# The last step of the inverse transform: three packed products of 128 rows in place of four of 96

## The chip, the core and the metric

The kernel runs on one core of one Trainium2 chip. The metric is the device time of one launch in microseconds. The kernel before takes 2950.87 us, the median of three runs (2947.91 to 2956.71).

## The reference

Two stages follow each other. The first filters a sequence of 3008 tokens of 256 channels in the frequency domain, for 8 batches; the second is a gated feed-forward layer over all 24064 tokens.

```python
X = np.fft.rfft(x, axis=1)                      # x: (8, 3008, 256)
y = np.fft.irfft(X * (filt_r + 1j * filt_i)[None], n=3008, axis=1).astype(np.float32)
t = y.reshape(8 * 3008, 256)
g = t @ w_gate                                  # (256, 1536)
v = t @ w_val                                   # (256, 1536)
out = (g / (1 + np.exp(-g)) * v) @ w_out        # (1536, 256)
```

All is in fp32 on the chip; the feed-forward weights come as float64 and are rounded to fp32 in the kernel.

## The kernel before

The transform of length 3008 = 47 x 64 is done in stages of small products: stage 1 over 47, stages 2a and 2b over 64 (with the filter between them), stage 3 over 47 back to tokens. Stages 1 and 2 of batch b+1, and stage 3 of the batch at hand, are laid as small pieces between the feed-forward products of batch b. All instructions of an engine stand in a fixed order.

A batch has four chunks of 752 tokens, each of two tiles of 376. A group is one chunk with one of three parts of the hidden width; so a batch has 4 x 3 = 12 groups. Stage 3 makes the tokens `y` of a chunk in four steps: two tiles `i`, each for two halves `cb` of the channels. Its input `t4` comes from DRAM, where stage 2b has put 48 rows (24 frequencies, real and imaginary) for each of 64 residues:

```python
N1, N2 = 47, 64
NS = 24
NR = 2 * N1          # 94 outputs of a pair of residues
NK = 4 * NS          # 96 rows of a pair: two blocks of 48
NH = 4               # pairs in a tile
TH = NH * NR         # 376
...
# the table of the last step, for a pair of residues h = 0, 1: block-diagonal, columns of the two mixed
wi = np.zeros((NS, 2, 2, N1, 2))
for h in range(2):
    wi[:, :, h, :, h] = v.transpose(2, 0, 1) / S
...
self.d2_rows = self.d2.rearrange("a (h n) c -> (a h) n c", h=2)    # d2: (48, 64, 256) in DRAM
...
def load(self, **kw):
    pin(nc.sync.dma_start(**kw))

def load_t4(self, k, i, part=None):
    if part is not None:
        ...                                     # first chunk of batch 0: into another buffer, in two parts
    else:
        t = t4pool.tile([NK, NH, C], FP32, name=f"t4_{self.b}_{k}_{i}", tag="t4")   # two buffers
        self.load(out=t, in_=self.d2_rows[:, ts(2 * k + i, NH), :])
    self.t4[k, i] = t

def stage3(self, k, step):
    if step == 0:
        self.y[k] = ypool.tile([128, 8, TQ], FP32, name=f"y_{self.b}_{k}", tag="y")
    i, cb = divmod(step, 2)
    ps = (self.bank if k == 0 else fbank)(f"pd_{self.b}_{k}_{step}")
    psv = ps.rearrange("p a b -> p (a b)")[:, 0:TH].rearrange("p (n r) -> p n r", n=NH)
    for n in range(NH):
        pin(nc.tensor.matmul(out=psv[:, n, :],
                             lhsT=self.t4[k, i][:, n, ts(cb, 128)],   # 96 x 128, stationary
                             rhs=wi_t, start=n == 0, stop=True,       # 96 x 94, moving
                             skip_group_check=True))
    yield
    ...                                         # ScalarE and VectorE copy and combine psv into y
```

Half of `wi_t` is zero: it takes both residues of a pair at once, and its columns come out in the order in which the tokens are wanted.

The loads of `t4` stand in SyncE's queue with everything else that it loads: the feed-forward weights of the next group (`wt_t`, four pieces a group, each rewritten when its last product is done), the input `x` of a later batch, filters and tables:

```python
chunk = {0: 1, 2: 2, 5: 3}.get(step)            # at the start of groups 0, 2 and 5 of a batch
if b and chunk:
    for i in range(2):
        cur.load_t4(chunk, i)
...
if nxt and (step, op) == (10, "A12" if b else "E23"):
    for i in range(2):
        nxt.load_t4(0, i)                       # the next batch's first chunk, in group 10
...
def reload_weights(g, piece):
    a, b = PIECES[piece]
    tc.keep_in_program_order(nc.sync.dma_start(out=wt_t[:, a:b], in_=w_dram[g, :, a:b]))
```

ScalarE starts the stores of stages 1 and 2b (`nc.scalar.dma_start`), between its copies.

The feed-forward products that surround these steps are of 188 and of 128 columns:

```python
for z in range(2):                              # lines 732 and 811 of the whole kernel
    pin(nc.tensor.matmul(out=ps[:, z], lhsT=self.wt[:, SLOT[p], z], rhs=rhs, ...))      # 128 x 188
...
pin(nc.tensor.matmul(out=self.tiles[at][:, t, :], lhsT=self.hs[i][:, HID[p], t0:t0 + 128],
                     rhs=wo_t[:, JB * q + i, WO[p], :], ...))                           # 128 x 128
```

Of the kernel before, what the change touches and what calls it, by code (L numbers as in the profile page):

```python
# [41 lines left out]
FP32 = mybir.dt.float32  # L42
# [6 lines left out]
B, S, C = 8, 3008, 256  # L49
# [4 lines left out]
N1, N2 = 47, 64  # L54
NS, NQ = 24, 64
NR = 2 * N1
NK = 4 * NS

NH = 4
# [50 lines left out]
PIECES = ((0, 7), (7, 14), (14, 20), (20, 26))  # L110


def dft_tables():
    n1, n2 = np.arange(N1), np.arange(N2)
    s, q = np.arange(NS), np.arange(NQ)
    ph = 2 * np.pi * (np.outer(n1, s) % N1) / N1
    w = np.stack([np.cos(ph), -np.sin(ph)], 1)
    wf = np.zeros((N1, 2, NS, 2, 2))
    wi = np.zeros((NS, 2, 2, N1, 2))

    v = np.stack([2 * np.cos(ph), -2 * np.sin(ph)], 0)
    v[0, :, 0], v[1, :, 0] = 1.0, 0.0
    for h in range(2):
        wf[:, h, :, :, h] = w.transpose(0, 2, 1)
        wi[:, :, h, :, h] = v.transpose(2, 0, 1) / S


    kap = np.where(q[:, None] < 32, s + N1 * q[:, None], s + N1 * (95 - q[:, None]))
    sg = np.where(q < 32, 1.0, -1.0)[:, None]
    th = 2 * np.pi * ((n2[:, None, None] * kap) % S) / S  # L130
    c, sn = np.cos(th), np.sin(th)
    d = np.zeros((2, N2, NS, 2, NQ))
    d[0, :, :, 0] = c.transpose(0, 2, 1)
    d[1, :, :, 0] = sn.transpose(0, 2, 1)
    d[0, :, :, 1] = (-sn * sg).transpose(0, 2, 1)
    d[1, :, :, 1] = (c * sg).transpose(0, 2, 1)
    d = d.reshape(128, NS, 128)
    de = np.stack([d, d.transpose(2, 1, 0)], 2)
    f32 = np.float32
    return (wf.reshape(NR, NK).astype(f32), wi.reshape(NK, NR).astype(f32),  # L140
            np.ascontiguousarray(de).astype(f32))


@with_exitstack
def kernel(
# [8 lines left out]
    out: bass.AP,  # L154
):
    nc = tc.nc
    wf_host, wi_host, de_host = dft_tables()
    wf_dram = nc.inline_tensor(wf_host, name="wf_tbl")
    wi_dram = nc.inline_tensor(wi_host, name="wi_tbl")
    de_dram = nc.inline_tensor(de_host, name="de_tbl").ap()  # L160
    unit_dram = nc.inline_tensor(np.eye(128, dtype=np.float32), name="unit_tbl")

    def pool(name, bufs, space=None):
        kw = {} if space is None else {"space": space}
        return ctx.enter_context(tc.tile_pool(name=name, bufs=bufs, **kw))

    cpool = pool("consts", 1)
    xpool = pool("xp", 2)
    t1pool = pool("t1", 2)
    t4pool = pool("t4", 2)  # L170
# [4 lines left out]

    wf_t = cpool.tile([NR, NK], FP32)
    wi_t = cpool.tile([NK, NR], FP32)

    wt_t = cpool.tile([128, NPR, 2, 128], FP32)
    y_t = cpool.tile([128, 3 * len(PAIRS), TQ], FP32)  # L180
# [25 lines left out]
    one = cpool.tile([128, 1], FP32)  # L206
# [15 lines left out]
    pin = tc.keep_in_program_order  # L222

    def add(eng, dst, a, b):
        return eng.tensor_tensor(out=dst, in0=a, in1=b, op=ALU.add)  # L225
# [50 lines left out]
    def load_weights(i):  # L276
        if i in raws or i >= len(weights):
            return
        if i < N_EARLY:
            raws[i] = early_raw(i)  # L280
        elif spot_of(i) is not None:
            raws[i] = bits(4 * 7 * 128 + 512 * spot_of(i))
        else:
            raws[i] = rpool.tile([128, 2, 128, 2], U32, name=f"raw_{i}", tag="raw", bufs=2)
        pin(nc.sync.dma_start(out=raws[i], in_=weights[i][0]))
# [169 lines left out]
    def bank(name):  # L455
        return wps.tile([128, 512], FP32, name=f"w{name}", tag="w")
# [4 lines left out]
    def idle(t, banks, n):  # L461

        for ps in banks:
            pin(nc.tensor.matmul(out=ps[:, 0:n], lhsT=t[:, 0:128], rhs=t[:, 0:n],
                                 start=True, stop=True))

    class Spectral:
# [59 lines left out]
        def load_t4(self, k, i, part=None):  # L527
            if part is not None:

                t = f0[0:NK, ts(i, NH), :]  # L530
                r = (slice(0, 64), slice(64, NK))[part]
                self.load(out=t[r], in_=self.d2_rows[r, ts(i, NH), :])
            else:
                t = t4pool.tile([NK, NH, C], FP32, name=f"t4_{self.b}_{k}_{i}", tag="t4")
                self.load(out=t, in_=self.d2_rows[:, ts(2 * k + i, NH), :])
            self.t4[k, i] = t

        def bank(self, name):
# [93 lines left out]
# [4 lines that stand above are left out]
            i, cb = divmod(step, 2)  # L636
            ps = (self.bank if k == 0 else fbank)(f"pd_{self.b}_{k}_{step}")
            psv = ps.rearrange("p a b -> p (a b)")[:, 0:TH].rearrange("p (n r) -> p n r", n=NH)
            for n in range(NH):
                pin(nc.tensor.matmul(out=psv[:, n, :],  # L640
                                             lhsT=self.t4[k, i][:, n, ts(cb, 128)],
                                             rhs=wi_t, start=n == 0, stop=True,
                                             skip_group_check=True))
            yield

            y = self.y[k]

            def tokens(part, parts):
                return y[:, part:part + parts].rearrange("p t (r n) -> p n (t r)", n=NH)

            if cb == 0:
                pin(nc.scalar.copy(out=tokens(2 * i, 2), in_=psv))
                return
            for t in range(2):
                a, c = 2 * i + t, psv[:, :, ts(t, N1)]
                b, v, k = tokens(a, 1), tokens(4 + a, 1), KS[a]
                if k == 0:
                    pin(nc.scalar.copy(out=v, in_=c))
                elif k == -1:
                    pin(add(nc.vector, v, c, b))  # L660
                else:
                    pin(nc.vector.scalar_tensor_tensor(
                        out=v, in0=b, scalar=-float(k), in1=c, op0=ALU.mult, op1=ALU.add))
# [172 lines left out]
    def run(piece):  # L836
        for _ in piece:
            pass

    with tc.tile_pool(name="start", bufs=1) as spool0:  # L840
# [12 lines left out]
        n = 0  # L853
# [34 lines left out]
        for u in range(N_TWO + lag):  # L888
            if u < N_TWO:
                spec.turn(u + 2)  # L890
                step = spec.stage2a(u)
                next(step)
                next(step)
                preparation.tick(0, 2 * (u < N_TWO - 2), hold=True)
                run(step)
                preparation.release()
                spec.real_part(u + 1)
            if u >= lag:
                if u == N_TWO:
                    idle(zero, [bank("idle")], 512)  # L900
                elif u > N_TWO:
                    preparation.tick(0)
                run(spec.stage2b(u - lag))
            if u == 6:
                pin(nc.sync.dma_start(out=wi_t, in_=wi_dram.ap()))
                for i in range(8, N_EARLY):
                    load_weights(i)
            if u == N_TWO - 1:
                for i in range(2):
                    spec.load_t4(0, i, 0)  # L910
# [7 lines left out]
        for p in ("A13", "A01"):  # L918
            at = SLOT[p]
# [32 lines left out]
    def order_of(b):  # L952

        steps = [divmod(step, NG) for step in range(NCHUNK * NG)]
        if b == 0:
            steps[:NT * NG] = [(k, g) for g in range(NG) for k in range(NT)]
        return steps
# [44 lines left out]
    for b in range(B):  # L1002
# [8 lines left out]
        one = [nxt.stage1(u) for u in range(N_ONE)] if nxt else []  # L1011
# [24 lines left out]
        for step in range(NCHUNK * NG + (b == B - 1)):  # L1036
            ghost = step == NCHUNK * NG
            k, g = order_of(b)[min(step, NCHUNK * NG - 1)]
# [15 lines left out]
            for place, token in enumerate(SCHEDULE):  # L1054
# [5 lines left out]
                if op[0] == "t":  # L1060
                    n = int(op[1])
                    ps = pieces_before if old else pieces
# [59 lines left out]
```

## Time and profile before

| what | before |
|---|---|
| span of the profiled run | 2946.9 us |
| TensorE busy, records | 2911.7 us, 20264 |
| weight loads | 2816.1 us |
| VectorE, ScalarE, GpSimd busy | 1929.3, 1609.9, 1579.8 us |
| mean granted TensorE clock | 0.998 |
| records of stage 3's products (`pd`, line 640) | 992, of 128.3 us busy |
| loads of `t4` through SyncE | 62, of 384 KB each |
| all DMA packets, bytes | 217452, 558.57 MB |

In the profile PE is TensorE's products, PEld its weight loads, DVE VectorE, ACT ScalarE, POOL GpSimd and SPq the queue in which SyncE starts its DMAs. Every fp32 product leaves two records of each kind. Names of tiles stand without buffer numbers: `t` is `t4`, `d` the DRAM tensors between the stages, `pd` the result of stage 3, `pa`, `pb` and `pc` those of stages 1, 2a and 2b, `wk`, `wa`, `we` those of the hidden products and `wA`, `wF`, `wG` those of the output products. Busy times of overlapping records add up to more than the time that they take, so the distance between two starts on the timeline says more than a length.

### The profile page before, as it was taken

How to read it: one execution, taken by the hardware profiler on the slowest of the kernel's cores; microseconds unless marked ns; L12 is line 12 of the kernel's file. 1: busy time of each engine (PE TensorE's matmuls, PEld its weight loads, DVE VectorE, ACT ScalarE, POOL GpSimd, SP SyncE). 2: the span in 40 equal slices, each digit the busy share in tenths (PEclk: the TensorE clock that was granted, in tenths of full speed). 3: DMA queues.
4: the chain of work that ended last, by engine and by line, in shares of the span. 5: the costliest groups of instructions: out<-in, count | busy, mean ns of one | idle time of the engine just before them, and what ended most of it. 6: DMA issues, size and time to landing. Idle time of an engine off the chain costs nothing.

```text
span 2946.9 us, 57623 instructions
## 1 busy us (share of the span) xinstructions
PE 2911.7 (99%) x20264; PEld 2816.1 (96%) x20264; DVE 1929.3 (65%) x4384; ACT 1609.9 (55%) x4208; POOL 1579.8 (54%) x1759
## 2 busy tenths in 40 slices
PE   7999999999999999999999999999999999999999
PEld 5889999999999999999999999999999999999999
DVE  6888765576655676557765667656666566766666
ACT  6775455545555555555455554555555555555554
POOL 3876655556444655455554456454564545555453
PEclk9999999999999999999999999999999999999999
DMA  8677855575555655556646566556665565644442
GB/s 232 212 255 245 299 188 184 174 229 180 178 179 185 222 186 171 182 188 200 213 152 194 188 195 212 162 176 203 194 199 171 177 211 190 201 138 152 148 129 88
DMA packets 217452, 558.57 MB, mean 190 GB/s; under 512 B 29962, under 2 KB 107642, under 8 KB 217166
## 3 DMA queue, kind: packets, MB, share of 16 engines
q1 hardware_dynamic: 171326, 485.59, 51.5%
q10 hardware_dynamic: 36912, 45.43, 4.6%
q0 software_dynamic: 8928, 23.89, 2.3%
q8 instruction: 162, 2.65, 0.4%
q14 instruction: 124, 1.02, 0.1%
HBM read 459.73 MB, written 95.05 MB: 188 GB/s over the span
## 4 chain that ended last, share of the span: by engine, by line
PE 94%; DVE 1%; POOL 1%; DMA 1%; issue 0%; ACT 0%; SPq 0%; DVEq 0%; POOLq 0%
PE wa L732 24%; PE wA L811 17%; PE wk L732 16%; PE we L732 12%; PE wG L811 9%; PE wF L811 4%; PE pd L640 4%; PE pa L548 3%; PE pc L620 2%; PE pb L588 2%; DMA y_t<-yt 0%; POOL y_t L225 0%; DVE h L779 0%; POOL wt_t L225 0%; POOL wt_t L228 0%
## 5 line engine op out<-in xcount | busy, mean ns | idle before, releaser
L732 PE MATMUL wa<-y_t,wt_t 128*128 128x188 f32 x4464 | 880.2, 323 | 5.2 <-issue 1.4
L732 PEld LDWEIGHTS wa<-y_t,wt_t 128*128 128x128 f32 x4464 | 730.0, 190 | 30.1 <-issue 17.3
L225 POOL TENSOR_TENSOR h<-h 128x376 f32<-128x376 f32 x190 | 183.1, 985 | 787.1 <-DVE h L779 777.5
L811 PE MATMUL wA<-wo_t,h 128*128 128x128 f32 x4608 | 577.7, 275 | 2.5 <-DVE o L225 2.0
L811 PEld LDWEIGHTS wA<-wo_t,h 128*128 128x128 f32 x4608 | 562.9, 192 | 16.2 <-issue 10.4
L732 PE MATMUL wk<-y,wt_t 128*128 128x188 f32 x2976 | 567.9, 324 | 0.0
L228 POOL TENSOR_TENSOR h<-h 128x376 f32<-128x376 f32 x570 | 553.5, 993 | 0.5
L732 PEld LDWEIGHTS wk<-y,wt_t 128*128 128x128 f32 x2976 | 479.2, 191 | 25.9 <-issue 19.8
L228 DVE TENSOR_TENSOR we<-we,m 128x376 f32<-128x376 f32 x576 | 318.6, 556 | 196.9 <-PE we L732 138.4
L732 PE MATMUL we<-y_t,wt_t 128*128 128x188 f32 x2232 | 431.5, 323 | 1.4 <-ACT we L763 1.4
L732 PEld LDWEIGHTS we<-y_t,wt_t 128*128 128x128 f32 x2232 | 369.4, 190 | 1.8 <-ACT we L763 1.7
L228 POOL TENSOR_TENSOR D<-f,f 128x376 f32<-128x376 f32 x288 | 281.0, 989 | 104.6 <-ACT f L747 103.9
L232 DVE SCALAR_TENSOR_TENSOR y<-wk,c 128x376 f32<-128x376 f32 x480 | 245.1, 543 | 133.8 <-ACT we L763 83.2
L767 ACT COPY m<-wa 128x376 f32<-128x376 f32 x576 | 272.0, 472 | 88.2 <-PE wa L732 87.0
L774 ACT ACTIVATE g<-wa 128x188 f32<-128x188 f32 x576 | 188.1, 327 | 190.6 <-PE wa L732 182.6
L811 PE MATMUL wG<-wo_t,h 128*128 128x128 f32 x2304 | 288.3, 275 | 0.6 <-DVE o L225 0.6
L811 PEld LDWEIGHTS wG<-wo_t,h 128*128 128x128 f32 x2304 | 281.4, 192 | 0.8 <-DVE o L225 0.8
L774 ACT ACTIVATE u<-we 128x188 f32<-128x188 f32 x576 | 189.0, 328 | 168.8 <-DVE we L228 149.9
L747 ACT ACTIVATE f<-wk 128x376 f32<-128x376 f32 x288 | 139.3, 484 | 235.4 <-PE wk L732 214.3
L751 ACT COPY c<-wk 128x376 f32<-128x376 f32 x288 | 136.0, 472 | 226.0 <-PE wk L732 226.0
L754 DVE SCALAR_TENSOR_TENSOR x<-wk,f 128x376 f32<-128x376 f32 x192 | 104.6, 545 | 235.8 <-PE wk L732 230.0
L763 ACT COPY we<-y 128x376 f32<-128x376 f32 x480 | 224.1, 487 | 33.7 <-DVE h L779 14.7
(142 smaller groups left out, 3915.9 us busy)
## 6 DMA issues: line engine op xcount, KB each, us to landing
wt_t<-w_all SPq DMA_DIRECT2D x174, 896.0 KB
wt_t<-w_all SPq DMA_DIRECT2D x174, 768.0 KB
t<-d SPq DMA_DIRECT2D x62, 384.0 KB
d<-t ACTq DMA_DIRECT2D x112, 192.0 KB
lent<-de_tbl SPq DMA_DIRECT2D x84, 256.0 KB
lent<-in_filt_r_dram SPq DMA_DIRECT2D x336, 64.0 KB
lent<-d SPq DMA_DIRECT2D x84, 256.0 KB
d<-lent ACTq DMA_DIRECT2D x84, 256.0 KB
```

What stands on the lines that cost most here:

```text
L225: return eng.tensor_tensor(out=dst, in0=a, in1=b, op=ALU.add)
L228: return eng.tensor_tensor(out=dst, in0=a, in1=b, op=ALU.subtract)
L232: return nc.vector.scalar_tensor_tensor(out=dst, in0=a, scalar=-1.0, in1=b, op0=ALU.mult, op1=ALU.subtract)
L640: pin(nc.tensor.matmul(out=psv[:, n, :], lhsT=self.t4[k, i][:, n, ts(cb, 128)], rhs=wi_t, start=n == 0, stop=True, skip_group_check=True))
L732: pin(nc.tensor.matmul(out=ps[:, z], lhsT=self.wt[:, SLOT[p], z], rhs=rhs, start=start and z == 0, stop=True, skip_group_check=True))
L747: pin(act.mul(self.small(f"f{i}", f"f{i}", 1), t[f"k{i}"], -1.0))
L751: pin(act.copy(out=self.small(f"c{i}", f"c{i}", 1), in_=t[f"k{i}"]))
L754: pin(v.scalar_tensor_tensor(out=dst, in0=t[f"k{j}"], scalar=-1.0, in1=t[f"f{i}" if j == 3 else f"D{at}"], op0=ALU.mult, op1=ALU.add))
L763: pin(act.copy(out=self.bank(f"e{at}"), in_=t[f"y{at}"]))
L767: pin(act.copy(out=self.small(f"m{at}", "m", 4), in_=t[f"a{at}"]))
L774: pin(act.activation(out=self.small(op, "g", 3, 1)[:, 0], in_=ps[:, 1], func=AF.Silu))
L811: pin(nc.tensor.matmul(out=self.tiles[at][:, t, :], lhsT=self.hs[i][:, HID[p], t0:t0 + 128], rhs=wo_t[:, JB * q + i, WO[p], :], start=star ...
```

## The change

A tile of four pairs has eight blocks of 48 rows, 384 rows in all, and that is three times 128. The change packs them: three tiles of 128 rows, where two blocks are cut in two parts (32 and 16 rows) that lie in neighbouring tiles, and whose partial results TensorE adds up in PSUM. So three products with all 128 rows take the place of four with 96, and the zeros of the table go. A new table `back_t` holds, for each of the three tiles, the block-diagonal coefficients: 3, 4 and 3 blocks of 47 columns. The order of the tokens in PSUM is the same as before, so a product now writes every second element. The load of a tile, one DMA before, is seven: for each packed tile one with two whole blocks, and one for each part.

The first chunk of batch 0 keeps the old way (`back = self.b or k`). The table is loaded once, at the start.

```diff
+BACK = (((0, 0, 0, 48), (1, 48, 0, 48), (2, 96, 0, 32)),
+        ((4, 64, 0, 48), (5, 112, 0, 16), (2, 0, 32, 16), (3, 16, 0, 48)),
+        ((5, 0, 16, 32), (6, 32, 0, 48), (7, 80, 0, 48)))
+BACK_AT = (0, 3 * N1, 7 * N1)
...
+    one = wi[:, :, 0, :, 0].reshape(2 * NS, N1)
+    back = np.zeros((128, 10 * N1))
+    for tile_, first in zip(BACK, BACK_AT):
+        for i, (_, row, a, rows) in enumerate(tile_):
+            back[row:row + rows, first + N1 * i:first + N1 * (i + 1)] = one[a:a + rows]
...
+    back_t = cpool.tile([128, 10 * N1], FP32)
...
-                t = t4pool.tile([NK, NH, C], FP32, name=f"t4_{self.b}_{k}_{i}", tag="t4")
-                self.load(out=t, in_=self.d2_rows[:, ts(2 * k + i, NH), :])
+                t = t4pool.tile([128, len(BACK), C], FP32, name=f"t4_{self.b}_{k}_{i}", tag="t4")
+                n = (2 * k + i) * NH
+                for j, tile_ in enumerate(BACK):
+                    whole = [(blk, row) for blk, row, _, rows in tile_ if rows == 2 * NS]
+                    for blk, row, a, rows in tile_:
+                        if rows < 2 * NS:
+                            at = blk // NH * 32 + n + blk % NH
+                            self.load(out=t[row:row + rows, j], in_=self.d2[a:a + rows, at])
+                    (blk, row), (blk2, row2) = sorted(whole, key=lambda w: w[1])
+                    at, at2 = [z // NH * 32 + n + z % NH for z in (blk, blk2)]
+                    both = self.d2[:, at:at2 + 1:at2 - at]
+                    self.load(out=t[row:row + 4 * NS, j], in_=both.rearrange("a n c -> n a c"))
...
-            for n in range(NH):
+            flat = ps.rearrange("p a b -> p (a b)")
+            back = self.b or k
+            for j in range(len(BACK) if back else 0):
+                first = BACK_AT[j]
+                cols = back_t[:, first:first + N1 * len(BACK[j])]
+
+                if j == 1:
+                    rows = flat[:, 1:2 * 187 + 1].rearrange("p (z y) -> p z y", z=2)[:, :, ::2]
+                else:
+                    at = j // 2 * (2 * N1 + 1)
+                    rows = flat[:, at:at + 6 * N1 - 1:2]
+                pin(nc.tensor.matmul(out=rows, lhsT=self.t4[k, i][:, j, ts(cb, 128)], rhs=cols,
+                                     start=j == 0, stop=True, skip_group_check=True))
+            for n in range(0 if back else NH):
                 pin(nc.tensor.matmul(out=psv[:, n, :],
...
+                pin(nc.sync.dma_start(out=back_t, in_=back_dram.ap()))
```

## The prediction

> **What bounds the kernel now.** I read the page's totals first, then its chain that ended last:
>
> ```profile
> PE 2911.7 (99%) x20264; PEld 2816.1 (96%) x20264; DVE 1929.3 (65%) x4384; ACT 1609.9 (55%) x4208; POOL 1579.8 (54%) x1759
> PE wa L732 24%; PE wA L811 17%; PE wk L732 16%; PE we L732 12%; PE wG L811 9%; PE wF L811 4%; PE pd L640 4%; PE pa L548 3%; PE pc L620 2%; PE pb L588 2%; DMA y_t<-yt 0%; POOL y_t L225 0%; DVE h L779 0%; POOL wt_t L225 0%; POOL wt_t L228 0%
> ```
>
> TensorE is the chain; the product that the change touches (pd, line 640) holds 4% of it. Next the table of busy time by stretch, for the start and one whole batch (columns: stretch, length, then busy time and count of TensorE, its weight loads, VectorE, ScalarE and GpSimd, then clock, DMA share, GB/s):
>
> ```profile
> 0.00:100.00 100.00, 81.15 (x448) 64.05 (x449) 71.78 (x144) 66.29 (x144) 46.44 (x66) 0.98 0.81 222
> 820.00:1180.00 360.00, 360.00 (x2513) 349.38 (x2513) 229.22 (x525) 193.21 (x505) 188.81 (x204) 1.00 0.59 189
> ```
>
> Of a batch's 360 us TensorE is busy for 360.00, so in batches 1 to 7 every ns taken from TensorE's stream should come off the span, unless something new makes it wait. Only the start has idle time.
>
> A record's busy time is no measure here, as records overlap: I take the distance between starts. TensorE's timeline around one changed product (start, length, operation, records):
>
> ```profile
> 1019.63 1.50 PE L811 MATMUL wF<-wo_t,h 128*128 128x128 f32 x12
> 1020.96 1.03 PE L620 MATMUL pc<-lent 128*128 128x256 f32 x4
> ...
> 1026.35 0.80 PE L732 MATMUL wk<-y,wt_t 128*128 128x188 f32 x4
> 1026.99 1.03 PE L640 MATMUL pd<-wi_t,t 96*128 96x94 f32 x8
> 1027.85 1.53 PE L811 MATMUL wA<-wo_t,h 128*128 128x128 f32 x12
> 1029.22 0.80 PE L732 MATMUL wk<-y,wt_t 128*128 128x188 f32 x4
> ```
>
> Each product leaves two records. Width 128: 1.33 us for 12, so 111 ns a record. Width 188: 0.64 for 4, so 160 ns. Width 256: the 4 pc records take 0.87, some 216 ns. That is a straight line of about 0.81 ns per column and record. At 94 columns it would give 84 ns, but pd's 8 records take 0.86 us, and the 12 records after them 1.37 instead of 1.33: 0.89 to 0.90 us for 8, again 111 ns. So pd pays for 128 columns of weights whatever it streams: it stands on a floor.
>
> **What the Trainium skill says.** "TensorE: Matmul & The Clock Gate", section "LDWEIGHTS (loading the stationary operand)": a load's time goes with the columns of the stationary operand, not its rows. The trace agrees: the 96-row load of pd takes 193 ns, the 128-row load of wA 192. Its section "Back-to-back issue gap" says the spacing is set by both load and matmul; the floor above shows it. "PSUM — Partial Sum Buffer", section "Specifications (TRN2)", says of 8-byte cachelines: "any non-contiguous AP slows matmuls significantly". The new products write every second fp32 element; no product of the kernel before does so, so no trace here shows its size. "DMA: Bandwidth & Descriptors", section "Anatomy of one DMA — SWDGE (gpsimd) path", puts a fixed cost of about 2.0 us on a DMA; the output stores on GpSimd's queue land 2.3 to 2.5 us after issue, which agrees.
>
> **The change part by part.**
>
> *Products.* The four-block path stays for the first chunk of batch 0; the other 31 chunks of 4 steps, 124 steps, change. Each lost 4 products of 96 rows by 94 columns, half of them against zeros, and gets three of 128 rows with 141, 188 and 141 columns. Before: 8 records at 111 ns, 889 ns. After: 141 columns are 111 + 13 x 0.81 = 122 ns, above the floor; so 4 x 122 + 2 x 160 = 808 ns. More columns (470 for 376), but fewer loads: 81 ns less. 124 x 81 = **10.0 us** less on TensorE, 248 of 20264 records fewer. Nearly all of it lies in full batches (16 steps, 1.3 us of 360 each).
>
> *Loads of t4.* One load of 384 KB becomes seven, with runs of 1 KB for 4 KB. SyncE's queue, around the load of a batch's first chunk:
>
> ```profile
> 1118.06 0.32 SPq L376 DMA_DIRECT2D wt_t<-w_all  x1
> 1127.83 0.80 SPq L479 DMA_DIRECT2D t<-d  x2
> 1128.73 8.83 SPq L376 DMA_DIRECT2D wt_t<-w_all  x3
> ```
>
> An issue costs about 0.40 to 0.45 us. A chunk's two loads become 14, some 6.3 us for 0.9; 31 x 12 = 372 more issues are about 160 us of SyncE over the span. Does it delay TensorE? The tile of the load at 1127.83 is first used at 1140.36, 12.5 us later; the one at 807.10 at 821.96; those at 867.74 and 958.60 over 60 us later. The first half (7 issues, 3.2 us, plus 2.5 to land) is there after 5.7 us, the second after 8.9, and its use is 12 us behind the first's. The weight reloads behind them (line 376) start 5.4 us later; a piece is rewritten once its last product is done and first read some 22 us later by the order of the schedule, and 896 KB at 190 GB/s take 4.7 us, so some 12 us are left. All hidden.
>
> *ScalarE.* In the built program a DMA of SyncE or ScalarE takes one of eight semaphores in turn and waits for the DMA eight before it. With 14 loads in a row, the next one or two of ScalarE's stores wait for a small load that now goes out late. Load at 1167.12, ScalarE's next store at 1171.55: the load eight before is about the eighth or ninth of 14, out at 1167.1 + 8 x 0.45 = 1170.7, landed near 1173, so ScalarE stands still for about 1.5 us. It is busy 54% of the batch. I estimate up to 0.3 us on TensorE, perhaps 10 times in all: 2.5 us.
>
> *The start.* Chunk 1's loads go out at 70.99, first use 78.49; seven issues and landing end at 76.7, just in time, while the raw weight load behind (71.98) comes 5.4 us later and a second set at 94.02 does the same. TensorE waits here already. I take 1.5 us, and nothing for the new 240 KB table.
>
> Sum: -10.0 + 2.5 + 1.5 = -6.0 us: 2944.9.
>
> **The rivals.** (1) *The strided output slows the product.* If it doubled the record, a step would take 1616 ns for 889: +0.73 x 124 = +90 us, 3041. For it: the skill's sentence, and that the kernel before kept outputs contiguous at the price of zeros. Against: fp32 streams a column in 0.81 ns, about two clocks of 2.4 GHz (the rate in the skill's "Back-to-back issue gap"), so there may be time to write each element by itself; that is a guess. I give it one chance in six, and a smaller slowdown one in ten. (2) *The loads become the wait*: ScalarE's stop reaches TensorE in full, 1.5 us x 31 = 46 us, 2997. For it: SyncE's queue is in order and shared with weight reloads. Against: the slack above, and ScalarE's 46% idle time. (3) *The gain is hidden anyway*, as another engine is the bound: 2951. Against: 360.00 of 360. (4) *Narrow records cost less than I think*: if pd really costs only the 0.86 us seen, the saving is 52 ns x 124 = 6.4 us, and the result 2948.
>
> **Range and chances.** The most that can be won is 10 us, 0.3%, so faster by 2% is all but out. Low end: all 10 us and a little of the start, 2938. High end: a mild form of (1) or (2), 30 to 40 us. A loss over 2% (59 us) needs rival 1 nearly whole.
>
> **What would show it.** Right: pd's records 6 a step, at 4 x 122 + 2 x 160 ns between starts, a batch some 1.3 us shorter than before, TensorE still at 360 of 360. The strided write would show as pd records over 200 ns apart; the loads as TensorE waits after ScalarE, on t (pd waiting for a DMA) or on wt_t. A longer start alone would show in the first 150 us. I would be wrong if the spacing of pd isn't what the line through wider products gives.

## The result, and the profile after

The changed kernel takes 3054.65 us (median; 3052.44 to 3059.9) against 2951.31: a ratio of 1.0351, 95% interval 1.033 to 1.0372. It is slower by 103 us, far above the range that I gave.

The page of the changed kernel, its totals and its chain (the lines that answer to those of before):

```profile
PE 2933.3 (96%) x20016; PEld 2825.5 (93%) x20016; DVE 1931.9 (63%) x4384; ACT 1610.1 (53%) x4208; POOL 1579.5 (52%) x1759
PE wa L771 22%; PE wA L850 15%; PE wk L771 15%; PE we L771 11%; PE wG L850 8%; PE wF L850 4%; DMA t<-d 3%; PE pd L676 3%; PE pa L574 3%; PE pb L614 2%; DMA lent<-de_tbl 2%; PE pc L646 2%; DMA x<-in_x_dram 2%; DMA lent<-d 1%; SPq L495 1%; DMA d<-lent 1%
```

TensorE has 248 records fewer, as foreseen, and yet is busy for longer, and at 96% no longer all of the time. DMA holds 11% of the chain, where it held 1%: transfers of `t`, of `lent` (the tables and inputs of stage 2) and of `x` (the input of stage 1) stand in it now.

The products themselves did what they should. TensorE's timeline around one of them (start, length, operation, records):

```profile
1065.67 0.80 PE L771 MATMUL wk<-y,wt_t 128*128 128x188 f32 x4
1066.31 0.96 PE L676 MATMUL pd<-back_t,t 128*128 128x141 f32 x6
1067.11 1.50 PE L850 MATMUL wA<-wo_t,h 128*128 128x128 f32 x12
1068.45 0.80 PE L771 MATMUL wk<-y,wt_t 128*128 128x188 f32 x4
```

Six records take 0.80 us, where the four products took 0.86, and the twelve that follow take 1.34 in place of 1.37. That is the 808 ns of the prediction, so the strided output adds nothing to it that can be seen.

The time went into waits of TensorE. Its three largest, and its wait for `t` itself, in the view of who waited for whom (total us, times, longest):

```profile
PE pb L614 <- DMA lent<-d: 38.0, 8, 9.2
PE pa L574 <- DMA x<-in_x_dram: 24.1, 6, 4.1
PE wa L771 <- ACT m L806: 16.8, 14, 1.9
PE pd L676 <- DMA t<-d: 4.3, 3, 1.8
```

In the kernel before, no wait of TensorE comes to 5 us in all. One of the waits for `lent`, on the timeline with what follows it (in brackets the idle time before, and what ended it):

```profile
1010.03 0.80 PE L771 MATMUL we<-y_t,wt_t 128*128 128x188 f32 x4
1016.02 2.04 PE L614 MATMUL pb<-lent 128*128 128x256 f32 x4 [5.19 <-DMA lent<-d]
1017.86 1.46 PE L771 MATMUL wa<-y_t,wt_t 128*128 128x188 f32 x4
1019.11 1.11 PE L771 MATMUL we<-y_t,wt_t 128*128 128x188 f32 x4
1020.06 0.80 PE L771 MATMUL wa<-y_t,wt_t 128*128 128x188 f32 x4
```

The wait costs more than itself. After it the four pb records take 1.84 us to the next start in place of 0.87, the next four 1.25 and then 0.95 in place of 0.64: some 1.9 us more, until the pace is back. The table by stretch (columns as in the prediction) has the granted clock, third from the end, at about half in that time and back at full from 1020 on:

```profile
1016.00:1018.00 2.00, 1.98 (x5) 1.64 (x6) 0.00 (x0) 0.00 (x0) 0.00 (x0) 0.50 0.97 399
1018.00:1020.00 2.00, 2.00 (x9) 2.00 (x8) 1.74 (x3) 0.00 (x0) 0.00 (x0) 0.57 1.01 308
1020.00:1022.00 2.00, 2.00 (x18) 2.00 (x17) 1.16 (x3) 1.74 (x5) 1.08 (x2) 1.00 0.47 110
```

Over the whole span the mean granted clock falls from 0.998 to 0.985.

Why was the transfer late? SyncE's queue of the changed kernel ahead of that wait (start, length of the issue with its waits, transfer, number):

```profile
990.27 0.34 SPq L392 DMA_DIRECT2D wt_t<-w_all  x1
990.67 10.68 SPq L495 DMA_DIRECT2D t<-d  x14
1001.91 1.26 SPq L392 DMA_DIRECT2D wt_t<-w_all  x1
1003.22 2.03 SPq L495 DMA_DIRECT2D lent<-de_tbl  x1
1005.35 2.35 SPq L495 DMA_DIRECT2D lent<-in_filt_r_dram  x4
1009.85 2.55 SPq L495 DMA_DIRECT2D lent<-in_filt_i_dram  x2
1013.08 0.39 SPq L495 DMA_DIRECT2D lent<-d  x1
```

The 14 loads take 10.68 us, not 6.3, and the loads behind them go on slowly too. The last line is the transfer that TensorE waits for. SyncE's queue itself stands still for earlier loads of `t` (a DMA waits for the one eight before it), which it never does in the kernel before:

```profile
SPq L495 <- DMA t<-d: 66.8, 84, 2.1
```

So the place of the loss is plain; its cause may be the number of issues (theory A), the short runs of 1 KB (theory B), or the products and their order in time (theory C).

### The profile page after: what moved, and what is told of

The parts are those of the page before. It is cut to its first block, busy times and chain, and to the rows that moved or that the text cites. A ratio compares the mean times of both kernels' runs of the same rounds, so it can differ in the third digit from the quotient of the medians.

```text
span 3052.3 us, 57570 instructions
## 1 busy us (share of the span) xinstructions
PE 2933.3 (96%) x20016; PEld 2825.5 (93%) x20016; DVE 1931.9 (63%) x4384; ACT 1610.1 (53%) x4208; POOL 1579.5 (52%) x1759
## 2 busy tenths in 40 slices
DMA packets 238803, 558.84 MB, mean 183 GB/s; under 512 B 33326, under 2 KB 134942, under 8 KB 238514
## 4 chain that ended last, share of the span: by engine, by line
PE 85%; DMA 11%; DVE 1%; SPq 1%; POOL 1%; ACT 1%; issue 1%; ACTq 0%; DVEq 0%; POOLq 0%
PE wa L771 22%; PE wA L850 15%; PE wk L771 15%; PE we L771 11%; PE wG L850 8%; PE wF L850 4%; DMA t<-d 3%; PE pd L676 3%; PE pa L574 3%; PE pb L614 2%; DMA lent<-de_tbl 2%; PE pc L646 2%; DMA x<-in_x_dram 2%; DMA lent<-d 1%; SPq L495 1%; DMA d<-lent 1%
## 5 line engine op out<-in xcount | busy, mean ns | idle before, releaser
L771 PE MATMUL wa<-y_t,wt_t 128*128 128x188 f32 x4464 | 887.6, 325 | 19.2 <-ACT m L806 16.8
```

## The experiments

**One load a tile.** If the eight blocks of a tile lie one after another in DRAM, their 384 rows are just what the three packed tiles want, and one DMA brings them, in runs of 1 KB as in the changed kernel. Stage 2b then writes its rows in another order (the columns of its table are swapped to suit), which also makes its stores runs of 2 KB.

```diff
-    ...                                    # the seven loads
+    rows = self.d2.rearrange("(t m) a c -> t (m a) c", t=8)[2 * k + i]     # 384 successive rows
+    self.load(out=t, in_=rows.rearrange("(j p) c -> p j c", p=128))
```

> The packed products stay, but stage 2b's rows lie in DRAM so that a packed tile is 384 successive rows, and one DMA of 1 KB runs loads it. Theory A (the 14 issues of a chunk in SyncE's in-order queue hold up the loads of x and of stage 2 behind them): TensorE's waits of some 12 us a batch go, the saving of 0.06 to 0.09 us a step stays, some 8 to 11 us under the kernel before: 2940 to 2944. Theory B (the 1 KB runs in place of 4 KB make the transfers slow, whatever their number): about as slow as the changed kernel, 3040 to 3055. Theory C (the strided products are at fault, and the waits only follow): also above 3040.

Measured: 2940.68 us, ratio to the kernel before 0.9972 (0.9963 to 0.9982). The products keep their gain, and runs of 1 KB are not at fault: theories B and C fall. By theory A the next run had to be slow.

**The same rows, seven loads.** Only the number of DMAs differs from the run before.

```diff
-    self.load(out=t, in_=rows.rearrange("(j p) c -> p j c", p=128))
+    for j, cuts in enumerate(((0, 32, 128), (0, 16, 32, 128), (0, 32, 128))):
+        for a, z in zip(cuts, cuts[1:]):
+            self.load(out=t[a:z, j], in_=rows[128 * j + a:128 * j + z])
```

> The same order of rows in DRAM as in the run with one load, but the tile is loaded by seven DMAs of the sizes that the changed kernel has. Theory A: as slow as the changed kernel, 3040 to 3060, the number of DMAs being the only difference to the run with one load. Theory B: the same as the run with one load, whatever that is.

Measured: 2939.6 us, ratio 0.9969 (0.9956 to 0.9983). So seven DMAs of the same sizes cost nothing, and theory A falls as well. The queue of this run shows what differs:

```profile
955.85 7.22 SPq L496 DMA_DIRECT2D t<-d  x14
963.94 0.34 SPq L394 DMA_DIRECT2D wt_t<-w_all  x1
964.32 0.43 SPq L496 DMA_DIRECT2D lent<-de_tbl  x1
964.85 1.87 SPq L496 DMA_DIRECT2D lent<-in_filt_r_dram  x4
966.82 2.03 SPq L496 DMA_DIRECT2D lent<-in_filt_i_dram  x2
969.37 0.39 SPq L496 DMA_DIRECT2D lent<-d  x1
```

14 issues in 7.22 us, and `lent` right behind them: the queue bears the number. Nor does it wait once for a load of `t` here. In the changed kernel it was the transfers that were slow.

**The kernel before with seven loads.** Its four products of 96 rows stay.

```diff
-    self.load(out=t, in_=self.d2_rows[:, ts(2 * k + i, NH), :])
+    for j, cuts in enumerate(((0, 96), (0, 32, 48, 64, 96), (0, 96), (0, 96))):
+        for a, z in zip(cuts, cuts[1:]):
+            self.load(out=t[a:z, j], in_=self.d2_rows[a:z, n + j])
```

> The kernel before with its four products of 96 rows, contiguous outputs, but each tile loaded by seven DMAs of 1 KB runs (96, 32, 16, 16, 32, 96, 96 rows). Theory A, B: the loss without the saving, 3055 to 3070. Theory C: the time of the kernel before, 2951.

Measured: 2948.07 us, ratio 0.9995 (0.9986 to 1.0004): no loss. This alone looks like theory C, but the run with one load has ruled that out; it says again that seven loads of 1 KB runs are harmless.

**Two bursts.** The changed kernel, with the second tile's loads later in the group.

```diff
-    for i in range(2):
-        cur.load_t4(chunk, i)              # at the start of groups 0, 2 and 5
+    cur.load_t4(chunk, 0)                  # there
+    ...
+    cur.load_t4(chunk, 1)                  # at Q3; for the next batch's first chunk at E01
```

> The changed kernel with the seven loads of a chunk's second tile put off by some 13 us within the group, so that bursts of 14 become bursts of 7. Theory A: a burst of 7 lasts some 3.2 us, about what the loads behind it can bear; the waits fall to less than half, 2945 to 2990. Theory B: no great change, since as many bytes and runs are moved: 3030 to 3055.

Measured: 2956.11 us, ratio 1.0023 (1.0016 to 1.003). Most of the waits go: TensorE is idle for 46.5 us of the span (2952.8 - 2906.3), in the changed kernel for 119.0. It suits any cause that grows with what is in flight at once, so it does not single out the number of issues.

**Theory D: the number of DMA engines.** What is left is the form of the two-block loads, which the slow kernel shares only with the run of two bursts: 96 rows that the transfer describes as 2 x 48. The Trainium skill, "DMA: Bandwidth & Descriptors", section "Why a DMA increments its semaphore by 16 and not by 1", says that a transfer is dealt to the largest number of engines, up to 16, that divides the slowest dimension of both sides, on SyncE's queue to the lowest-numbered ones, and that each posts one increment when done. If each increment is a small packet, it is among the packets under 512 B that the page of a run counts. The kernel before, then the changed kernel:

```profile
DMA packets 217452, 558.57 MB, mean 190 GB/s; under 512 B 29962, under 2 KB 107642, under 8 KB 217166
```

```profile
DMA packets 238803, 558.84 MB, mean 183 GB/s; under 512 B 33326, under 2 KB 134942, under 8 KB 238514
```

If all seven loads of a tile ran on 16 engines, the changed kernel would have 62 x 6 x 16 = 5952 small packets more (the run with seven loads has just 36058 - 30106 = 5952 more than the one with a single load). It has 3364 more: 62 x (4 x 16 + 3 x 2 - 16) = 3348, and 16 for the table. So by the count the four parts use 16 engines, the three two-block loads **two**. The DMA share bears it out. In the changed kernel, late in the 14 loads (columns as in the prediction; the last three are clock, DMA share and GB/s):

```profile
1000.00:1001.00 1.00, 1.00 (x11) 1.00 (x10) 0.97 (x2) 0.00 (x0) 1.00 (x2) 1.00 0.13 44
```

Two engines of 16 are a share of 0.125. Of a chunk's two tiles, 288 KB fall to each of the two. The whole kernel moves 558.57 MB in 58.9% of 16 engines' 2946.9 us (the sum of the queues' shares), 20 KB a us and engine; so two engines have, as an estimate, some 14 us of work. Every transfer behind that is dealt to all 16 needs those two for its own share. The trace does not name a packet's engine, so that it is always the same two rests on the skill. The run of two bursts fits: it has the same 33326 small packets, but one tile's 144 KB at a time, some 7 us by the same estimate, and lost 0.2%.

**Pairs apart.** The changed kernel, each two-block load as two of 48 rows: ten DMAs a tile, all on 16 engines.

```diff
-    both = self.d2[:, at:at2 + 1:at2 - at]
-    self.load(out=t[row:row + 4 * NS, j], in_=both.rearrange("a n c -> n a c"))
+    for z, r in ((at, row), (at2, row2)):
+        self.load(out=t[r:r + 2 * NS, j], in_=self.d2[:, z])
```

> The changed kernel, but each load of two whole blocks (96 rows that the transfer describes as 2 x 48) is issued as two loads of 48 rows: ten DMAs a tile for seven, nothing else. Theory D (a transfer is dealt to as many of the 16 DMA engines as divide its outermost dimension, so the 2 x 48 loads run on the same two engines, and all later loads, which need those two as well, land late): the loss goes, 2938 to 2955, though 20 issues a chunk in place of 14 make a longer burst. Theory A (number of issues in SyncE's queue): slower than the changed kernel, above 3060.

Measured: 2955.22 us, ratio 1.0022 (1.0013 to 1.0031). Three more DMAs a tile take 99 us off, and SyncE's queue no longer waits for a load of `t`: theory D. It stays above the run with one load by 14.5 us. The number of issues is the likely reason, since 20 of them hold the queue as long as the 14 slow ones did; no run isolates it, and the run with one load also stores in longer runs.

```profile
959.59 10.82 SPq L495 DMA_DIRECT2D t<-d  x20
...
978.70 0.39 SPq L495 DMA_DIRECT2D lent<-d  x1
```

Of the 8.3 us between the end of the 20 issues and the last line, the queue waits 3.3 for a store that ScalarE began at 975.25 (`d<-lent`). TensorE waits about once a batch for pb, up to 2.6 us (1.68 us at 981.44).

**The kernel before on two engines.** One load of 384 KB a tile in runs of 4 KB, with the old products. Only the order of the rows is another (2 x 48), with the rows of the table to suit; the first chunk of batch 0 is loaded in eight parts in place of four.

```diff
-    self.load(out=t, in_=self.d2_rows[:, ts(2 * k + i, NH), :])            # "(a h) n c"
+    rows = self.d2.rearrange("a (h n) c -> h a n c", h=2)
+    self.load(out=t, in_=rows[:, :, ts(2 * k + i, NH), :])
```

> The kernel before with its four products and one load of 384 KB in runs of 4 KB a tile, but the rows of a tile stand as 2 x 48 in place of 96 (and those of the table accordingly), so that the transfer's outermost dimension is 2. Theory D: 192 KB on each of two DMA engines for a tile, more than the 144 KB of the changed kernel; 3020 to 3150. Theories A and B (issues, short runs): 2951, as the kernel before.

Measured: 3104.76 us, ratio 1.0525 (1.0503 to 1.0547). With the same number and sizes of products, no further DMA in the batches and no short runs, the loss is there, and larger; 192 KB a tile fall to each of two engines, for 144. The table by stretch after the two loads of a chunk (issued at 1005.42):

```profile
1009.00:1014.00 5.00, 5.00 (x36) 4.92 (x35) 3.38 (x7) 2.71 (x7) 4.88 (x6) 1.00 0.13 52
1021.00:1027.00 6.00, 2.68 (x21) 2.39 (x19) 0.00 (x0) 0.05 (x1) 0.98 (x1) 1.00 0.14 55
```

For these 11 us the DMA share is that of two engines, and in the second stretch TensorE stands still for more than half of the time. The count of small packets:

```profile
DMA packets 216648, 558.57 MB, mean 180 GB/s; under 512 B 29158, under 2 KB 106838, under 8 KB 216362
```

804 fewer than before: 62 x (2 - 16) = -868, and the four more DMAs at the start, of 16 each, give +64.

**The same order of rows in halves.** The control to it.

```diff
     rows = self.d2.rearrange("a (h n) c -> h a n c", h=2)
+    for h in range(2):
+        self.load(out=t[48 * h:48 * h + 48], in_=rows[h, :, ts(2 * k + i, NH), :])
```

> The same order of rows as the run with the 2 x 48 load, but as two loads of 48 rows. Theory D: 2951, as the kernel before. If the order of rows itself cost something, the loss of the 2 x 48 run would stay.

Measured: 2948.09 us, ratio 0.9992 (0.9983 to 1.0001). The order of the rows costs nothing; carrying it in one transfer of 2 x 48, and not in two of 48, costs 157 us.

**Contiguous outputs.** The run with one load, each product writing successive elements. The results stand at other places, and some columns of neighbouring tiles are added; the time of the products is what counts.

```diff
-    rows = flat[:, at:at + 6 * N1 - 1:2]       # and the like for the middle tile
+    at = (0, 118, 235)[j]
+    rows = flat[:, at:at + N1 * len(BACK[j])]
```

> The run with one load, with the three products writing successive elements in PSUM (the results then stand at other places than the reference's; some columns of neighbouring tiles are added). If the stride of two elements costs nothing: 0.80 us a step as before, 2940, the same as the run with one load. If it costs part of what the packing saves: under 0.78 us a step, below 2936.

Measured: 2937.54 us, ratio 0.9963 (0.9952 to 0.9975), whose interval overlaps that of the run with one load. The timeline decides, contiguous:

```profile
1022.77 0.80 PE L763 MATMUL wk<-y,wt_t 128*128 128x188 f32 x4
1023.41 0.96 PE L668 MATMUL pd<-back_t,t 128*128 128x141 f32 x6
1024.21 1.50 PE L842 MATMUL wA<-wo_t,h 128*128 128x128 f32 x12
```

0.80 us for the six records, as with the stride. TensorE's busy time, 2901.3 us against 2902.5, is 1.2 us less over all 124 steps.

## Why the prediction was wrong

*Products: right.* 808 ns a step foreseen, 0.80 us measured, and without the loads' fault the run with one load is 8.3 us faster than the kernel before, of the 10.0 worked out (rival 3, no gain at all, is out). Its interval, some 5 to 11 us, does not exclude the 6.4 of rival 4; TensorE's busy time, 9.2 us less (2911.7 - 2902.5), speaks for the 10.0. Rival 1, the strided output, to which I gave one chance in six, is refuted: no cost of it can be seen here. That a loss over 2% needed rival 1 nearly whole was wrong too.

*Loads of t4: wrong, the step that failed.* "All hidden" rested on two things. First, I took each of the seven loads for a transfer like any other, 0.45 us to issue and 2.5 to land. Three of them are dealt to two of 16 engines, and a chunk's 14 took 10.68 us (up to 19 in other chunks) before the last was out. The rule was at hand, and I read only the number and the size of the loads, not how each describes its rows. Second, I checked the slack of `t4` itself and of the weights behind it, but not of the other loads in the same queue. Of those TensorE waits most: the inputs of stage 2 (38.0 us) and `x` (24.1 us), which the kernel loads only a unit or two ahead. `t4`, with its 12 us, is waited for during 4.3 us in all.

*ScalarE: right in kind, too small.* It did come to wait for late loads, most ahead of a copy (c), where neither the kernel before nor the run with seven loads in one order has such a wait:

```profile
ACT c L790 <- DMA t<-d: 26.3, 7, 4.0
```

I put 2.5 us on TensorE; it waited 16.8 us for ScalarE's copies (m), in 14 places of 1.2 us on average, against 1.2 us in the kernel before. That ScalarE is late there because its stores stood behind late loads is by the order of the semaphores; no run isolates it.

*The sum.* Against the run with one load, which has the same products and 2937.7 us of profiled span, the changed kernel's span is longer by 114.6 us. TensorE's idle time (span less busy) accounts for 3052.3 - 2933.3 = 119.0 less 2937.7 - 2902.5 = 35.2, so 83.8 us; its longer busy time, 2933.3 - 2902.5, for 30.8 us. The products are the same, so I put this down to the slower pace after waits, as on the timeline above; the mean clock, 0.985 for 0.999, fits. The prediction had no term for that second part.

*Rival 2* named the right place, the loads, with a bound of 46 us from ScalarE's stop alone. It was the right rival by the wrong way, and less than half of the size.

The version to keep is the one with one load: 0.9972 of the time before. With seven loads in the same order of rows it is as fast (0.9969).

## What to carry to other kernels

When a change splits or re-describes a transfer, look at the outermost dimension of both sides as the DMA carries it, not only at bytes, runs and number: 2 x 48 rows ran on two engines of 16, 96 rows or twice 48 on all. Two things in a profile showed it here: the count of small packets, one for each engine that takes part in a DMA, and stretches with a DMA share of 0.13 to 0.14 after the loads. And when a queue gets longer, ask for the slack of everything behind in that queue, above all of what is loaded a unit or two ahead, and add the slow clock after each wait of TensorE to its price.

## What the runs showed of the hardware that I had not expected

- A product that writes every second fp32 element in PSUM keeps the pace of a contiguous one: 0.80 us for six records, both ways. The Trainium skill, "PSUM — Partial Sum Buffer", section "Specifications (TRN2)", has it that such a pattern slows matmuls significantly; for these fp32 products the measurement decides against it.
- A tile's 384 KB as one DMA of 2 x 48 rows, in place of two DMAs of 48 with the same bytes at the same places, made the kernel 157 us slower (3104.76 against 2948.09).
- A wait of 5.19 us is followed by about 4 us in which the granted clock is 0.50 to 0.57 and TensorE's products take up to twice their time; over the changed kernel TensorE is busy for 30.8 us longer than with the same products and one load a tile.
